# Rebasing float64 weights to float32: a parametric ReLU on ScalarE and two VectorE steps in place of three or four

## The chip, the cores and the metric

The kernel runs on one core of a Trainium2 chip. The core has five engines that run side by side, each through its own instructions in a fixed order: TensorE (PE in the profile) for matrix products, VectorE (DVE), ScalarE (ACT) and GpSimd (POOL) for elementwise work, and SyncE (SP), whose queue issues the transfers between the chip's main memory and the on-chip memory. The metric is the device time of one execution in microseconds (us); lower is better.

## The reference

Eight batches of eight heads of attention with a local window and 32 global positions, and then a gated feed-forward network over the 4608 rows that come out:

```python
# attention, per batch and head: D = 64, Sl = 512 local and Sg = 32 global positions
k_all, v_all = concat(k_g, k_l), concat(v_g, v_l)
out_g = softmax(q_g @ k_all.T / 8) @ v_all
mask = abs(pos[:, None] - pos[None, :]) <= 32
s_l = concat(q_l @ k_g.T / 8, where(mask, q_l @ k_l.T / 8, -1e9))
out_l = softmax(s_l) @ v_all
x = concat(out_g, out_l)                      # as (4608, 512)
# feed-forward: d_model = 512, d_ff = 1536
gate = 1.0 / (1.0 + np.exp(-(x @ w_gate)))
val = x @ w_val
return (gate * val @ w_out).astype(np.float32)
```

The three weight matrices are drawn as float32 and then multiplied by a float64 scalar, so they arrive as float64.

## The kernel before

**Weights.** A float64 weight reaches the kernel as two 32-bit words: `high` (sign, 11 bits of exponent, upper 20 bits of mantissa) and `low` (the rest). The kernel makes a float32 of the two, and splits that into a rounded part `hi` and a remainder `lo`, which TensorE multiplies in its faster float32 format in three passes (hi·hi, lo·hi, hi·lo).

There are 36 pieces to convert, 12 blocks f of each of w_gate, w_val and w_out, in the order gate, val, out for f = 0, 1, ... A piece is a tile of 128 x 1024 words, and its words become 128 x 512 float32. The sources are loaded by SyncE into three buffers in turn (`stage`, line 126; `in_w_gate_dram`, `in_w_val_dram` and `in_w_out_dram` in the profile); the load for piece i + 3 is issued after piece i has been read. The results `v` have two buffers in turn. All five buffers are parts of one tile, called `xt` in the profile, as the tiles are that hold the input of the feed-forward.

`convert(i, hi, lo)` does these steps, all on `high` and `low` with a stride of two words:

1. L137, VectorE: `v = high & 0x80000000`, the sign.
2. L141 on ScalarE for odd i, or L143 on VectorE for even i: `high`, read as a float32, is multiplied in place by 2^-112. Read so, the upper 8 of the 11 exponent bits are a float32's exponent, and the multiplication takes 112 from them, which takes 896 = 1023 - 127 from the float64's exponent.
3. L144, VectorE: `v = (low >> 29) | v`, the lowest three bits of the mantissa.
4. L145, VectorE: `v = (high << 3) | v`. The shift drops the sign and the two exponent bits that are zero by now.
5. L146, ScalarE: `hi = round(v)`; L147, GpSimd: `lo = v - hi`. For gate and val these go to the resident tiles `wg` and `wv`; for out they go to two temporary tiles and from there by SyncE to main memory (`wo_dram`, L158 and L159), from which every block is loaded again (L433) when it is used.

**Work around it.** The rows are taken in chunks: 256 rows, 256 rows, then seven chunks of 512, and the 256 global rows last. Attention for a chunk runs ahead of the feed-forward of that chunk, mixed into the feed-forward of earlier chunks. One unit of local attention is: scores on TensorE (`bank_x`, L239), mask and maximum on VectorE (L253), exponential on ScalarE (L256, also its sum), reciprocal on VectorE (L259, L260), normalisation into `p_buf` (L223 on VectorE or L221 on ScalarE), transposes on TensorE (`bank_y`, L275), a copy of them on ScalarE (`pt_nat`, L283, in the first chunks), the product with the values on TensorE (L298, L299), and a copy of the result on ScalarE (L302). Global positions have the like (L323 to L361). The feed-forward of one block f is 12 matmuls for the gate (`bank_g`, L405), 12 for the value (`bank_v`, L405), tanh, exponential and absolute value on ScalarE (L413 to L420), two VectorE steps (L425, L426), the split into `hh` (L428 ScalarE, L429 VectorE), and the product with w_out (`bank_o`, L442). While the first chunk's attention runs alone, `fill` (L110) issues matmuls of no use that keep TensorE going.

**Order.** The kernel keeps a queue of events by due time, counted in units of four 512-column matmuls, and emits those that are due between the feed-forward's groups of matmuls. Conversions of block 0 come during the first chunk's attention, the others at four units a block:

```python
CONVERT = (-2, 4, 1, 3)
CONVERT_EARLY = (-985, -980, -977)
```

From what is emitted, the framework's planner, which has costs of its own for every instruction, fixes the order on each engine and sets the waits. `tc.issue_after(x)` tells it to put the instructions inside the block behind x on x's engine; for the first three pieces, `convert` does so with `anchor[0]`, the last masked score (L253) emitted, which is on VectorE.

Of the kernel before, what the change touches and what calls it, by code (L numbers as in the profile page):

```python
# [11 lines left out]
AF = mybir.ActivationFunctionType  # L12
ALU = mybir.AluOpType
# [38 lines left out]
REBASE = "vs"  # L52
# [7 lines left out]
def kernel(ctx, tc, qk, v, w_gate, w_val, w_out, out_l, out_g):  # L60
    nc = tc.nc
# [60 lines left out]
    def stage(i):  # L122
        if i < len(w_src):
            src = w_src[i]
            st = conv_bufs[0][i % len(conv_bufs[0])].rearrange("p (t n) -> p t n", t=src.shape[1])
            nc.sync.dma_start(st, src)

    def convert(i, hi, lo):

        src = w_src[i]  # L130
        t, n = src.shape[1], src.shape[2] // 2
        st, v = (o[i % len(o)].rearrange("p (t n) -> p t n", t=t) for o in conv_bufs)
        words = st.rearrange("p t (n two) -> p t n two", two=2)
        low, high = words[:, :, :, 0], words[:, :, :, 1]
        vf, hf = v.bitcast(F32), high.bitcast(F32)
        with tc.issue_after(anchor[0].ins) if i < 3 else nullcontext():
            nc.vector.tensor_scalar(v, high, 0x80000000, None, op0=ALU.bitwise_and)  # L137


            if REBASE[i % len(REBASE)] == "s":  # L140
                nc.scalar.mul(hf, hf, 2.0 ** -112)  # L141
            else:
                nc.vector.tensor_scalar(hf, hf, 2.0 ** -112, None, op0=ALU.mult)  # L143
            nc.vector.scalar_tensor_tensor(v, low, 29, v, op0=ALU.logical_shift_right, op1=ALU.bitwise_or)  # L144
            nc.vector.scalar_tensor_tensor(v, high, 3, v, op0=ALU.logical_shift_left, op1=ALU.bitwise_or)  # L145
        nc.scalar.copy(hi, vf)  # L146
        nc.gpsimd.tensor_tensor(lo, vf, hi.bitcast(F32), op=ALU.subtract)  # L147
        stage(i + len(conv_bufs[0]))

    def convert_w(f, i):  # L150
        fs = slice(f * P, (f + 1) * P)
        w = (wg, wv)[i]
        convert(3 * f + i, w[0][:, :, fs], w[1][:, :, fs])

    def convert_wo(f):
        hi, lo = (spl.tile([P, 1, DM], F32R, name=nm, tag="kl") for nm in ("wo_hi", "wo_lo"))
        convert(3 * f + 2, hi, lo)
        nc.sync.dma_start(wo_dram[f][:, 0], hi[:, 0].bitcast(F32))  # L158
        nc.sync.dma_start(wo_dram[f][:, 1], lo[:, 0].bitcast(F32))  # L159
# [463 lines left out]
```

## Time and profile before

| | |
|---|---|
| runs: median (lowest to highest of 3) | 1196.94 us (1195.49 to 1201.54) |
| the profiled execution | 1196.95 us, with a span of 1195.2 us from its first to its last instruction |
| TensorE busy | 1154.4 us, 97% of the span |
| weight loads of TensorE (PEld) | 967.4 us, 81% |
| VectorE busy | 808.8 us, 68% |
| ScalarE busy | 746.6 us, 62% |
| GpSimd busy | 416.6 us, 35% |
| mean granted clock of TensorE | 0.992 of full |
| moved by DMA | 151.81 MB, 127 GB/s in the mean |

The profile's lines name the source line (L144), the engine, the operation, the tile written and, behind the arrow, those read. A group's line ends with its busy time, the mean of one in ns, and the idle time of the engine just before, with what ended it. "A <- B" in a list of waits says that A waited and B let it go. The queue of an engine carries a q (SPq is SyncE's). The granted clock is the share of its full clock that TensorE was given.

### The profile page before, as it was taken

The page shows a single profiled execution, that of the slowest core. Times are in us where ns is not written, and L with a number is a line of the kernel's source. Part 1 is how long each engine was busy: PE and PEld are TensorE (multiplying, and loading weights), DVE is VectorE, ACT ScalarE, POOL GpSimd, SP SyncE. Part 2 cuts the span into 40 slices and gives each one's busy share as a digit, 9 for nine tenths or more (in the row PEclk, how much of TensorE's full clock was granted, in tenths as well). Part 3 has the DMA queues.
Part 4 walks back from the last instruction along what each step waited for, and adds up shares of the span by engine and source line. Part 5 has one row for each costly group of instructions (what it writes and reads, how often), then busy time and mean ns, then how long its engine had stood idle before and what let it go on. Part 6 is the DMA issues. An engine that isn't in the chain of part 4 may idle for free.

```text
span 1195.2 us, 19155 instructions
## 1 busy us (share of the span) xinstructions
PE 1154.4 (97%) x6596; PEld 967.4 (81%) x6596; DVE 808.8 (68%) x2186; ACT 746.6 (62%) x1719; POOL 416.6 (35%) x408
## 2 busy tenths in 40 slices
PE   8889999999999999999999999999999999999998
PEld 6667778888888888888888888888888888888897
DVE  6989966766776776766776776667676677633343
ACT  4776777756765676766676666666665666532333
POOL 1335344524442444424443444434443443100000
PEclk9899999999999999999999999999999999999999
DMA  8787854333433443434333433443343342132143
GB/s 289 240 258 230 261 173 136 114 101 98 123 95 119 126 111 88 123 119 114 99 111 115 123 98 108 114 128 96 114 114 102 114 114 67 53 106 64 61 145 120
DMA packets 59489, 151.81 MB, mean 127 GB/s; under 512 B 6144, under 2 KB 19456, under 8 KB 59392
## 3 DMA queue, kind: packets, MB, share of 16 engines
q1 hardware_dynamic: 59392, 150.59, 41.8%
q8 instruction: 52, 0.85, 0.3%
q14 instruction: 45, 0.37, 0.1%
HBM read 135.36 MB, written 15.20 MB: 126 GB/s over the span
## 4 chain that ended last, share of the span: by engine, by line
PE 76%; DVE 13%; ACT 6%; issue 3%; DMA 1%; POOL 0%; ACTq 0%; SPq 0%; DVEq 0%; POOLq 0%
PE bank_v L405 20%; PE bank_g L405 20%; PE bank_o L442 19%; PE bank_x L239 4%; DVE p_buf L223 4%; PE bank_y L275 4%; ACT s_sb L256 2%; PE bank_x L323 2%; PE bank_x L306 2%; PE bank_x L307 2%; PE bank_x L366 1%; DVE bank_v L425 1%; DVE bank_v L426 1%; DVE mn L418 1%; DVE t L310 1%
## 5 line engine op out<-in xcount | busy, mean ns | idle before, releaser
L405 PE MATMUL bank_v<-xt,wv 128*128 128x512 f32 (+1 forms) x1440 | 329.9, 366 | 14.1 <-DVE pt L287 14.1
L405 PE MATMUL bank_g<-xt,wg 128*128 128x512 f32 (+1 forms) x1440 | 332.3, 366 | 0.6 <-ACT pg_buf L327 0.6
L442 PE MATMUL bank_o<-wo,hh 128*128 128x512 f32 x1224 | 328.9, 400 | 0.9 <-ACT hh L428 0.5
L405 PEld LDWEIGHTS bank_v<-xt,wv 128*128 128x128 f32 x1440 | 238.9, 191 | 51.3 <-issue 16.2
L405 PEld LDWEIGHTS bank_g<-xt,wg 128*128 128x128 f32 x1440 | 238.4, 190 | 38.1 <-issue 3.1
L442 PEld LDWEIGHTS bank_o<-wo,hh 128*128 128x128 f32 x1224 | 217.1, 189 | 40.7 <-ACT hh L428 1.4
L256 ACT ACTIVATE s_sb<-s_sb,nm 128x192 f32<-128x192 f32 (+1 forms) x240 | 110.4, 461 | 100.5 <-DVE nm L253 99.6
L223 DVE TENSOR_SCALAR p_buf<-s_sb,r 128x128 f32<-128x128 f32 (+2 forms) x443 | 154.8, 386 | 6.1 <-PE bank_y L275 1.7
L311 POOL TENSOR_TENSOR x<-t 64x256 f32<-64x256 f32 x104 | 76.4, 735 | 172.4 <-DVE t L310 148.4
L216 POOL TENSOR_TENSOR vhl<-v_raw,vhl 128x512 fp32r<-128x512 f32 x52 | 67.2, 1293 | 187.8 <-ACT vhl L215 88.1
L203 POOL TENSOR_TENSOR kl<-qk_raw,qk_hi 128x704 fp32r<-128x704 f32 x52 | 88.6, 1705 | 108.2 <-ACT qk_hi L202 107.7
L428 ACT CAST hh<-bank_v 128x512 fp32r<-128x512 f32 (+1 forms) x120 | 62.7, 523 | 95.4 <-DVE bank_v L426 94.6
L413 ACT ACTIVATE th<-bank_g 128x512 f32<-128x512 f32 (+1 forms) x120 | 63.9, 532 | 88.0 <-PE bank_g L405 87.5
L418 DVE TENSOR_SCALAR mn<-bank_g 128x512 f32<-128x512 f32 (+1 forms) x108 | 67.5, 625 | 72.3 <-ACT th L413 72.3
L310 DVE TENSOR_TENSOR t<-bank_x,t 64x512 f32<-64x512 f32 x104 | 70.7, 680 | 62.1 <-ACT t L309 61.1
L425 DVE TENSOR_TENSOR bank_v<-bank_v,mn 128x512 f32<-128x512 f32 (+1 forms) x120 | 73.6, 614 | 51.5 <-PE bank_v L405 48.2
L253 DVE CUSTOM_DVE_ANT_0 s_sb<-bank_x,masks 128x192 f32<-128x192 f32 (+1 forms) x240 | 80.0, 370 | 38.1 <-PE bank_x L239 35.1
L429 DVE TENSOR_TENSOR hh<-bank_v,hh 128x512 fp32r<-128x512 f32 (+1 forms) x120 | 73.0, 608 | 34.8 <-ACT hh L428 32.7
L205 POOL TENSOR_TENSOR qk_hi<-qk_raw,qk_hi 64x256 fp32r<-64x256 f32 x104 | 80.2, 792 | 4.1
L275 PE MATMUL bank_y<-ident,p_buf 128*128 128x128 f32 x440 | 70.7, 276 | 6.5 <-DVE p_buf L223 5.6
L426 DVE SCALAR_TENSOR_TENSOR bank_v<-th,bank_v 128x512 f32<-128x512 f32 (+1 forms) x120 | 73.2, 610 | 1.6
L275 PEld LDWEIGHTS bank_y<-ident,p_buf 128*128 128x128 f32 x440 | 54.8, 141 | 22.6 <-DVE p_buf L223 5.7
(110 smaller groups left out, 1694.6 us busy)
## 6 DMA issues: line engine op xcount, KB each, us to landing
wo<-wo_dram SPq DMA_DIRECT2D x116, 512.0 KB, 3.4
qk_raw<-in_qk_dram SPq DMA_DIRECT2D x104, 312.0 KB, 4.5
v_raw<-in_v_dram SPq DMA_DIRECT2D x52, 256.0 KB, 2.6
out_dram<-ob SPq DMA_DIRECT2D x34, 256.0 KB, 3.0
xt<-in_w_gate_dram SPq DMA_DIRECT2D x12, 512.0 KB, 4.8
xt<-in_w_val_dram SPq DMA_DIRECT2D x12, 512.0 KB, 4.6
xt<-in_w_out_dram SPq DMA_DIRECT2D x12, 512.0 KB, 4.7
v_nat<-in_v_dram SPq DMA_DIRECT2D x8, 512.0 KB, 6.2
```

Source lines behind the costliest of these rows:

```text
L203: nc.gpsimd.tensor_tensor(kl, t[:, K0:Q1], hi[:, K0:Q1].bitcast(F32), op=ALU.subtract)
L205: nc.gpsimd.tensor_tensor(hi[64:128, r], t[64:128, r], hi[64:128, r].bitcast(F32), op=ALU.subtract)
L223: nc.vector.tensor_scalar(out, in_, by, None, op0=ALU.mult)
L253: anchor[0] = nc.vector.tensor_tensor_reduce(out=s_sb[:, i, w], in0=s_ps[:, i, w], in1=mid[:, w], scale=-0.125, scalar=3.0e38, op0=ALU.add ...
L256: exp_at[0] = nc.scalar.activation(s_sb[:, i, w], s_sb[:, i, w], AF.Exp, bias=nm[:, i:i + 1], scale=-1.0, accum_out=sm[:, i:i + 1])
L275: nc.tensor.transpose(pt_ps[:, t], flat[:, t * P:(t + 1) * P], ident)
L310: nc.vector.tensor_tensor(t0, o_ps[0:64], t0, op=ALU.add)
L405: nc.tensor.matmul(acc, w[a][:, t, fs], xt[:, c, t, x0:x0 + ntok], start=n == 0, stop=n == 11)
L418: nc.vector.tensor_scalar(mn, acc, 0.0, None, op0=ALU.min)
L425: nc.vector.tensor_tensor(acc, acc, mn, op=ALU.mult)
L426: nc.vector.scalar_tensor_tensor(acc, th, 1.0, acc, op0=ALU.add, op1=ALU.mult)
L442: nc.tensor.matmul(o_ps[t], ph[:, a, t * P:(t + 1) * P], pwo[:, c], start=f2 == 0 and i == 0, stop=f2 == NF - 1 and i == 2)
```

## The change

Steps 1 and 3 above lose the sign, and step 2 runs on ScalarE for every piece. It is a parametric ReLU: it scales `high` by 2^-112 and, where the result is negative, multiplies by -2^32. That leaves a positive number whose 8 exponent bits are 32 higher than without the sign; 32 is bit 28 of the word, and the shift by 3 of step 4 lifts it to bit 31, the sign of a float32. So `v` starts as `low >> 29`, with no OR. The ReLU stands ahead of the `issue_after` block. What follows (L146, L147, the next load) is as it was; the number of transfers is too.

```diff
         vf, hf = v.bitcast(F32), high.bitcast(F32)
+        nc.scalar.activation(hf, hf, AF.Prelu, scale=2.0 ** -112, alpha=-2.0 ** 32)
         with tc.issue_after(anchor[0].ins) if i < 3 else nullcontext():
-            nc.vector.tensor_scalar(v, high, 0x80000000, None, op0=ALU.bitwise_and)
-
-
-            if REBASE[i % len(REBASE)] == "s":
-                nc.scalar.mul(hf, hf, 2.0 ** -112)
-            else:
-                nc.vector.tensor_scalar(hf, hf, 2.0 ** -112, None, op0=ALU.mult)
-            nc.vector.scalar_tensor_tensor(v, low, 29, v, op0=ALU.logical_shift_right, op1=ALU.bitwise_or)
+            nc.vector.tensor_scalar(v, low, 29, None, op0=ALU.logical_shift_right)
             nc.vector.scalar_tensor_tensor(v, high, 3, v, op0=ALU.logical_shift_left, op1=ALU.bitwise_or)
         nc.scalar.copy(hi, vf)
         nc.gpsimd.tensor_tensor(lo, vf, hi.bitcast(F32), op=ALU.subtract)
```

## The prediction

> **What bounds the kernel now.** I read the page first, then the stretches of the run, then TensorE's waits in the one stretch that the change touches, then the groups of VectorE and ScalarE there.
>
> ```profile
> span 1195.2 us, 19155 instructions
> ...
> PE   8889999999999999999999999999999999999998
> ...
> DVE  6989966766776776766776776667676677633343
> ```
>
> Each digit is a fortieth of the span, about 30 us. TensorE (PE) is at 9 nearly throughout: a TensorE-bound kernel. Only its first three digits are 8, and there VectorE (DVE) reads 9 8 9 9 behind its first 6, against 6 and 7 later. That is where the weights are converted. The next view gives stretches in us; its columns are TensorE, weight loads, VectorE, ScalarE and GpSimd busy time (instructions), then the granted clock, the DMA share and GB/s.
>
> ```profile
> 20.00:40.00 20.00, 16.47 (x97) 12.23 (x95) 19.35 (x57) 13.31 (x34) 7.15 (x7) 0.90 0.69 229
> 40.00:60.00 20.00, 19.76 (x107) 15.17 (x107) 17.32 (x45) 15.39 (x45) 7.81 (x7) 0.84 0.74 241
> ...
> 80.00:100.00 20.00, 18.23 (x97) 13.89 (x96) 15.42 (x38) 14.74 (x42) 7.16 (x6) 0.83 0.64 208
> ...
> 20.00:160.00 140.00, 125.81 (x786) 97.03 (x785) 127.28 (x317) 101.81 (x281) 56.03 (x43) 0.94 0.76 244
> ...
> 300.00:1000.00 700.00, 685.86 (x3787) 575.02 (x3787) 494.54 (x1371) 465.86 (x1023) 288.78 (x285) 1.00 0.39 111
> ```
>
> From 20 to 160 us TensorE stands idle for 140 - 125.81 = 14.2 us, while VectorE is busy for 127.28 of 140 (91%) and ScalarE for 101.81 (73%). In 300 to 1000 us, with VectorE at 71% (494.54 of 700) and ScalarE at 67%, TensorE idles 2%: nothing to win there by this change, which touches nothing there. There is a second loss in the early stretch, the clock: 0.10 of 16.47, 0.16 of 19.76 and 0.17 of 18.23 make 1.6 + 3.2 + 3.1 = 7.9 us that TensorE would not need at full clock. So the most that the stretch can give is 14.2 + 7.9 = 22.1 us, and the floor is about 1175 us. Who makes TensorE wait in 20 to 160 us (total us, times, longest):
>
> ```profile
> PE bank_y L275 <- DVE p_buf L223: 5.6, 5, 2.2
> PE bank_x L298 <- ACT pt_nat L283: 3.1, 4, 1.8
> PE bank_y L345 <- DVE r L259: 1.5, 1, 1.5
> PE bank_x L298 <- ACT pt_first L283: 0.7, 1, 0.7
> PE bank_g L405 <- ACT pg_buf L327: 0.6, 1, 0.6
> PE bank_y L275 <- ACT pg_buf L327: 0.6, 1, 0.6
> PE bank_y L275 <- DVE p_first L223: 0.5, 1, 0.5
> PE bank_x L360 <- ACT ptg_nat L349: 0.5, 1, 0.5
> PE bank_o L442 <- ACT hh L428: 0.5, 1, 0.5
> PE bank_o L442 <- DVE hh L429: 0.4, 1, 0.4
> PE bank_y L275 <- ACT p_buf L221: 0.2, 1, 0.2
> ```
>
> VectorE ends 5.6 + 1.5 + 0.5 + 0.4 = 8.0 us of them, ScalarE 6.2 us; together all of the 14.2. None names a converted weight (wg, wv): TensorE never waits for a conversion itself, but for softmax steps that stand behind conversion steps in VectorE's order.
>
> **The change part by part.** The groups of the conversion in 20 to 160 us (busy us, mean ns), VectorE's four and ScalarE's:
>
> ```profile
> L145 DVE SCALAR_TENSOR_TENSOR xt<-xt 128x512 uint32<-128x512 uint32 x36 | 30.9, 860 | 1.1 <-ACT xt L141 0.5
> L144 DVE SCALAR_TENSOR_TENSOR xt<-xt 128x512 uint32<-128x512 uint32 x35 | 30.2, 862 | 0.2
> L137 DVE TENSOR_SCALAR xt<-xt 128x512 uint32<-128x512 uint32 x35 | 19.5, 558 | 4.0 <-POOL wv L147 2.3 <-POOL wo_lo L147 1.2 <-DMA xt<-in_w_val_dram 0.4
> L143 DVE TENSOR_SCALAR xt<-xt 128x512 f32<-128x512 f32 x17 | 10.1, 595 | 0.1
> ...
> L141 ACT ACTIVATE xt<-xt 128x512 f32<-128x512 f32 x18 | 12.3, 681 | 2.7 <-DVE xt L137 2.6
> L146 ACT CAST wg<-xt 128x512 fp32r<-128x512 f32 x12 | 7.4, 619 | 3.6 <-DVE xt L145 3.2
> ```
>
> *VectorE.* The mask (L137) becomes a shift of the low words: one tensor-scalar, same tile, same stride, so I take 558 ns again, no gain. It still waits for GpSimd's subtraction two steps back, since v has two buffers: the 2.3 + 1.2 us of waits in its row stay. L144 goes (30.2 us) and L143 goes (10.1 us). VectorE drops by 40.3, from 127.3 to 87.0 us.
>
> *ScalarE.* Today it multiplies in 18 of the 36 conversions (12.3 us); afterwards it runs a parametric ReLU in all 36, on the same strided tile, in place. No such instruction is in the trace. Nearest is L141 itself, an ACTIVATE with a scale on the same tile: 681 ns, which I take. The casts of the same size (619) bound it below; above I take the widest ACTIVATE, 128x544 with a bias column, 750 ns. So 36 x 0.681 = 24.5 us, 12.2 more than now (10.0 to 14.7); ScalarE goes from 101.8 to 114.0 us, 81% of 140, or 88% if the stretch shrinks to 130.
>
> ```profile
> L337 ACT ACTIVATE pg_buf<-pg_buf,mg 128x544 f32<-128x544 f32 x16 | 12.0, 750 | 1.8 <-DVE mg L336 1.8
> ```
>
> The Trainium skill (ScalarE: Activation LUTs, "Rules for kernel authors") speaks against this part: multiplies and ReLUs belong on VectorE. The rows agree on the price, 595 ns there against 681 here; the 17 moved multiplies would cost 17 x 0.086 = 1.5 us more in engine time by that rule, and the sum would only turn if VectorE had the idle time, which here it has not.
>
> *Waits.* The multiply waited for VectorE's mask (2.6 us of ScalarE's idle time in L141's row); the ReLU does not. One case of it is in the order of time (start, duration; idle before):
>
> ```profile
> 79.23 1.49 DVE L137 TENSOR_SCALAR xt<-xt 128x512 uint32<-128x512 uint32 x1 [1.16 <-POOL wv L147]
> ...
> 80.75 0.71 ACT L141 ACTIVATE xt<-xt 128x512 f32<-128x512 f32 x1 [1.99 <-DVE xt L137]
> ...
> 82.20 0.43 PE L298 MATMUL bank_x<-pt_nat,v_nat 128*64 128x128 f32 x2 [1.77 <-ACT pt_nat L283]
> ```
>
> GpSimd holds the mask, the mask holds ScalarE's multiply, behind which stands the copy of transposed probabilities (L283), for which TensorE waits 1.8 us; the clock then falls (0.83 in 80 to 100). That chain is cut. In exchange the ReLU is now the first to wait for the weight load, on ScalarE, with exponentials (L256), copies (L283, L302), tanh (L413) and the cast behind it, and VectorE's last step behind these. Today the first step waits for a load once, 0.4 us in L137's row, here:
>
> ```profile
> 111.73 0.38 SPq L126 DMA_DIRECT2D xt<-in_w_val_dram  x1
> ...
> 117.98 0.43 DVE L137 TENSOR_SCALAR xt<-xt 128x512 uint32<-128x512 uint32 x1 [0.39 <-DMA xt<-in_w_val_dram]
> ```
>
> The load took about 6.2 us from issue, VectorE ran late behind it, and TensorE's longest wait for p_buf, 2.2 us, follows. That one I leave in. No DMA is added or removed; a load is released by the conversion's last step, which comes about one L144 (0.86 us) sooner, so SyncE's queue gains a little, nothing that TensorE waits for. The ReLU also stands outside the ordering block of the first three conversions, so ScalarE may take it earlier in the first chunk of attention; at worst it holds one exponential for its own 0.68 us, three times, 2.0 us in all, at best nothing; I take nothing, as these fill copies of L110 run on TensorE there.
>
> *The sum.* (1) VectorE's 8.0 us of waits: all but the 2.2 go, since 40.3 of 127.3 us leave its order: 5.8 (bounds 3 to 8.0). (2) ScalarE's 6.2: the 1.8 goes; the rest grows with 12.2 us more work in the same order. If a sixth of that lands in front of something that TensorE needs, it costs 2.0 (bounds 0 and about 6, half of it; I stay low because TensorE now waits only 6.2 us for an engine at 73%): net -0.2. (3) Clock: 3.1 us of 80 to 100 go with their cause; of the 4.8 us in 20 to 60, which follow the first chunk's gaps (3.5 us idle in 20 to 40), I take a quarter, 1.2: 4.3 (bounds 1 to 7.9). Together 9.9 us. The profiled execution took 1196.95 us, 1.75 over its span and equal to the median of the runs (1196.94), so 1187.0 us.
>
> The Trainium skill (TensorE: Matmul & The Clock Gate, "Part 1: The HAM clock gate") says that the clock halves after an idle window of about 3.4 us. No gap in the rows is that long (longest 2.2), and the clock fell all the same; by the rule there would be nothing to recover and the sum would be 5.6 us, 1191.3, which is counted with rival A. The rows decide.
>
> **The rivals.**
> (A) Latency, not load: TensorE's waits are turns of the softmax loop, and ScalarE takes VectorE's place as the full engine. For it: 6.2 of the 14.2 us are ScalarE's already, at 73%. Against it: TensorE idles 2% in 300 to 1000 us with the same kind of loop and both engines near 70%. Half of the 8.0 goes (4.0), ScalarE takes 2.0 back, the clock gives 1: 1194, within the 0.5% (6 us, 1191 to 1203) that a measurement of this kernel can tell from no change.
> (B) Slower: ScalarE is held by weight loads. 36 conversions in 140 us are one per 3.9 us; with three buffers a load has two periods, 7.8 us, less the conversion in front. Against the median load of 4.6 us below that leaves about 3 us, against the 6.2 above next to nothing. It decides where loads take over 7.8 us: if half of the 36 hold ScalarE for 2.0 us, as L137 held it at 80.75, 36 us come on top of 114.0 and ScalarE needs 150 us for a stretch of 140: 10 us longer, 1207.
>
> ```profile
> xt<-in_w_val_dram SPq DMA_DIRECT2D x12, 512.0 KB, 4.6
> ...
> L256 ACT ACT_TABLE_LOAD x1 | 1.3, 1283 | 0.7 <-PEq L610 0.7
> ```
>
> (C) The parametric ReLU may not be in the table set that the exponentials and tanh share, which the program loads once. Two loads round each conversion are 72 x 1.283 = 92 us on ScalarE: 206 us for a stretch of 140, 66 us longer, 1263. Relu, abs, exp and tanh here share one load, which speaks against it. The Trainium skill (ScalarE: Activation LUTs, "Table sets: the hidden batching unit") names relu and abs as fillers of every set and does not name this function, and gives a switch 2.66 us with its drain, by which it would be worse.
> (D) More: all of VectorE's 8.0, the 1.8 and the whole 7.9 of clock, 17.7 us: 1179.
>
> **How the numbers follow.** Forecast 0.48 (its own range 1181 to 1191), A 0.27, B 0.11, C 0.03, D 0.11 (1175 to 1181). Faster by over 0.5%: 0.48 + 0.11 = 0.59; within: 0.27; slower: 0.14. The range 1177 to 1203 leaves out B, C and the lower third of D, 0.18. The point is the forecast's, 1187.
>
> **What would show it.** Right: L144's and L143's work gone, VectorE near 87 us of the stretch, one ScalarE activation of about 0.68 us per conversion, one table load, TensorE's waits for p_buf under 3 us, the clock at 1.00 in 80 to 100, and the conversions over some 10 us sooner. Wrong: ScalarE waiting for in_w loads (B), waits for ScalarE's copies grown by what VectorE's lost (A), a slow clock after the first chunk as before with no gap removed, or a ReLU much over 0.75 us.

## The result, and the profile after

The changed kernel takes 1187.33 us (median of 6 runs, 1185.29 to 1191.53), the kernel before 1197.34 us on the same chip (6 runs, 1195.49 to 1201.54). The ratio is 0.9916, with a 95% interval of 0.9893 to 0.994: 0.84% faster, 10 us. The profiled execution of the changed kernel took 1188.97 us, with a span of 1187.1 us, 8.1 less than the span before.

Lines of the changed kernel are 6 less than those of the kernel before from L145 on (L145 is now L139, L223 is L217, L405 is L399), the parametric ReLU is L136 and the shift that takes the mask's place L138. The page's head, and its slices of about 30 us:

```profile
span 1187.1 us, 19115 instructions
...
DVE  5767756666776676667776677677676677633343
ACT  5897777666666666666666666576665675532333
```

VectorE's first digits are 5 7 6 7 7 5 where they were 6 9 8 9 9 6. ScalarE's third is 9 now. The stretches of the changed kernel (TensorE, weight loads, VectorE, ScalarE, GpSimd busy; clock; DMA):

```profile
20.00:40.00 20.00, 17.45 (x112) 13.35 (x110) 16.56 (x48) 14.41 (x39) 8.90 (x8) 1.00 0.83 269
40.00:60.00 20.00, 19.20 (x120) 14.78 (x120) 13.30 (x42) 18.01 (x52) 7.61 (x8) 1.00 0.83 270
...
80.00:100.00 20.00, 18.15 (x106) 12.84 (x107) 12.38 (x36) 18.68 (x50) 6.94 (x7) 1.00 0.80 259
100.00:120.00 20.00, 18.02 (x123) 13.78 (x121) 14.28 (x35) 12.58 (x36) 8.35 (x7) 0.86 0.73 239
...
20.00:160.00 140.00, 130.62 (x845) 100.87 (x844) 98.31 (x273) 114.09 (x313) 56.59 (x47) 0.98 0.79 256
...
300.00:1000.00 700.00, 686.37 (x3788) 575.47 (x3787) 494.69 (x1373) 463.41 (x1018) 290.81 (x290) 1.00 0.38 111
```

In 20 to 160 us TensorE idles for 9.4 us instead of 14.2, and gets 845 matmul records done instead of 786. The clock is full up to 100 us, where three of these stretches were slow before (0.90, 0.84 and 0.83); it falls once, later, in 100 to 120. In 300 to 1000 us nothing has changed. That nearly everything was won early shows in the stores of the result, of the kernel before and of the changed one (the last two numbers are the start of the first and the last store):

```profile
L387 SPq DMA_DIRECT2D out_dram<-ob x34: 332/342/426, 246.5 to 1192.1; - x34
```
```profile
L381 SPq DMA_DIRECT2D out_dram<-ob x34: 332/360/433, 238.7 to 1184.0; - x34
```

The first is 7.8 us sooner, the last 8.1. Who makes TensorE wait in 20 to 160 us of the changed kernel:

```profile
PE bank_y L269 <- DVE p_buf L217: 2.7, 3, 1.1
PE bank_x L292 <- ACT pt_nat L277: 1.1, 1, 1.1
PE bank_y L269 <- ACT mn L409: 1.0, 1, 1.0
PE bank_o L436 <- ACT hh L422: 0.9, 1, 0.9
PE bank_y L339 <- DVE r L253: 0.8, 1, 0.8
PE bank_g L399 <- DVE hh L423: 0.8, 1, 0.8
PE bank_x L292 <- ACT pt_first L277: 0.7, 1, 0.7
PE bank_y L269 <- ACT p_buf L215: 0.5, 1, 0.5
PE bank_y L269 <- DVE hh L423: 0.2, 1, 0.2
PE bank_y L339 <- DVE pg_buf L217: 0.2, 1, 0.2
```

VectorE ends 4.7 us of them (8.0 before), ScalarE 4.2 (6.2 before). The steps of the conversion in the changed kernel, first VectorE's in the whole run, then ScalarE's by the source line (min/median/max in ns, first and last start):

```profile
L139 DVE SCALAR_TENSOR_TENSOR xt<-xt 128x512 uint32<-128x512 uint32 x36 | 30.0, 837 | 7.4 <-ACT xt L136 7.0
```
```profile
L138 DVE TENSOR_SCALAR xt<-xt 128x512 uint32<-128x512 uint32 x36 | 21.3, 596 | 11.7 <-POOL wo_lo L141 4.9 <-POOL wg L141 3.0 <-DMA xt<-in_w_gate_dram 1.8
```
```profile
L136 ACT ACTIVATE xt<-xt x36: 647/676/694, 8.7 to 145.3; 128x512 f32<-128x512 f32 x36
L136 ACT ACT_TABLE_LOAD  x1: 1283/1283/1283, 0.7 to 0.7; - x1
```

The ReLU costs what the multiplication did (676 ns), and one table load serves the program. Something that the prediction had seen only in part is at the very start. ScalarE in the kernel before, and in the changed one:

```profile
6.15 0.46 ACT L256 ACTIVATE s_first<-s_first,nm 128x192 f32<-128x192 f32 x1 [4.13 <-DVE nm L253]
```
```profile
8.69 0.68 ACT L136 ACTIVATE xt<-xt 128x512 f32<-128x512 f32 x1 [6.67 <-DMA xt<-in_w_gate_dram]
9.27 0.44 ACT L250 ACTIVATE s_first<-s_first,nm 128x192 f32<-128x192 f32 x1
```

The planner puts the first ReLU ahead of the first exponential. ScalarE waits there 6.67 us for the weight load, and the first exponential starts 3.1 us later than before. TensorE hardly feels it: its dummy matmuls (L110) run meanwhile, and its first product with the values (L298 before, L292 now) starts at 13.79 us, where it started at 13.34.

### The profile page after: what moved, and what is told of

Read it like the earlier page. It is cut to its first block, busy times and chain, and to the rows that moved or that the text cites. A ratio compares the mean times of both kernels' runs of the same rounds, so it can differ in the third digit from the quotient of the medians.

```text
span 1187.1 us, 19115 instructions
## 1 busy us (share of the span) xinstructions
PE 1150.8 (97%) x6596; PEld 963.8 (81%) x6596; DVE 776.9 (65%) x2132; ACT 755.0 (64%) x1737; POOL 412.4 (35%) x408
## 4 chain that ended last, share of the span: by engine, by line
PE 70%; DVE 10%; ACT 5%; issue 2%; POOL 1%; DMA 0%; ACTq 0%; DVEq 0%; POOLq 0%
PE bank_v L399 19%; PE bank_g L399 19%; PE bank_o L436 19%; DVE p_buf L217 4%; PE bank_y L269 3%; PE bank_x L233 3%; ACT s_sb L250 3%; PE bank_x L300 2%; PE bank_x L301 2%; PE bank_x L317 1%; PE bank_x L360 1%; DVE t L304 1%; DVE mn L412 1%; DVE bank_v L419 1%; DVE bank_v L420 1%
## 5 line engine op out<-in xcount | busy, mean ns | idle before, releaser
L399 PE MATMUL bank_v<-xt,wv 128*128 128x512 f32 (+1 forms) x1440 | 327.8, 364 | 14.7 <-DVE pt L281 14.4
L399 PE MATMUL bank_g<-xt,wg 128*128 128x512 f32 (+1 forms) x1440 | 331.1, 365 | 1.1 <-DVE hh L423 0.8
L399 PEld LDWEIGHTS bank_v<-xt,wv 128*128 128x128 f32 x1440 | 237.0, 189 | 51.8 <-issue 16.4
L399 PEld LDWEIGHTS bank_g<-xt,wg 128*128 128x128 f32 x1440 | 237.3, 189 | 38.7 <-issue 2.7
L217 DVE TENSOR_SCALAR p_buf<-s_sb,r 128x128 f32<-128x128 f32 (+2 forms) x443 | 152.4, 381 | 6.3 <-PE bank_y L269 1.7
L413 ACT ACTIVATE mn<-mn 128x512 f32<-128x512 f32 (+1 forms) x108 | 62.9, 582 | 15.8 <-DVE mn L412 11.1
```

Of the source, the lines that this page charges most:

```text
L217: nc.vector.tensor_scalar(out, in_, by, None, op0=ALU.mult)
L399: nc.tensor.matmul(acc, w[a][:, t, fs], xt[:, c, t, x0:x0 + ntok], start=n == 0, stop=n == 11)
```

## The experiments

The theory is the prediction's: TensorE waits early on for softmax steps that stand behind conversion steps in VectorE's order, and the gain is VectorE's shorter order ("load"). The rivals: the gain is that ScalarE's step no longer waits for VectorE's mask ("chain"); it is the planner's new order ("order"); it is TensorE's clock ("clock"). Ratios are to the kernel before on the same chip; the mean clock is that of a kernel's runs. The kernel before had 0.992 in each of the three sets of runs.

| kernel | median us (runs) | ratio (95% interval) | mean clock |
|---|---|---|---|
| changed | 1187.33 (6) | 0.9916 (0.9893 to 0.994) | 0.998 |
| or_again | 1195.22 (12) | 0.9972 (0.9957 to 0.9987) | 0.995 |
| scalar_twice | 1199.87 (12) | 1.0003 (0.9986 to 1.002) | 0.992 |
| mul_all_scalar | 1197.03 (12) | 0.9993 (0.9978 to 1.0007) | 0.994 |
| mul_all_vector | 1201.50 (12) | 1.0024 (1.0011 to 1.0037) | 0.991 |
| more_fill_before | 1205.28 (6) | 1.0048 (1.003 to 1.0066) | 0.994 |
| prelu_odd | 1195.94 (12) | 0.9973 (0.9959 to 0.9988) | 0.994 |
| prelu_late | 1179.82 (4) | 0.9836 (0.9816 to 0.9857) | 0.999 |
| norm_vector | 1186.75 (5) | 0.9887 (0.9869 to 0.9905) | 0.999 |
| shifted_before | 1198.97 (12) | 1.0002 (0.9982 to 1.0023) | 0.992 |
| shifted_after | 1188.99 (6) | 0.9921 (0.9898 to 0.9944) | 0.997 |
| late_or_again | 1198.46 (12) | 0.9999 (0.998 to 1.0018) | 0.992 |
| norm_late | 1184.04 (6) | 0.9879 (0.9854 to 0.9904) | 0.998 |

### VectorE's step put back (or_again)

```diff
             nc.vector.tensor_scalar(v, low, 29, None, op0=ALU.logical_shift_right)
+            nc.vector.scalar_tensor_tensor(v, low, 29, v, op0=ALU.logical_shift_right, op1=ALU.bitwise_or)
```

> The changed kernel with VectorE's OR-shift of the low words put back behind the plain shift (it gives the same words again). ScalarE's parametric ReLU stays, so nothing on ScalarE waits for VectorE's mask. VectorE gets back 36 instructions of about 0.86 us, 30 of the 40 us that the change took off it. Load theory (the gain is VectorE's order made shorter): three quarters of the loss of TensorE waits comes back, 1193 to 1197 us, and TensorE's waits for VectorE in 20 to 160 us go back over 6 us. Chain theory (the gain is that ScalarE's multiply no longer waits for VectorE): stays within 2 us of the changed kernel, 1186 to 1190.

Measured: ratio 0.9972, so 0.56% of the 0.84% is gone: 0.0056 x 1197 = 6.7 us for 30 us of VectorE. Its stretch from 20 to 160 us:

```profile
20.00:160.00 140.00, 125.56 (x808) 97.28 (x807) 120.81 (x302) 110.36 (x299) 59.17 (x45) 0.96 0.79 252
```

VectorE is at 120.8 us, and TensorE's idle time is back to 14.4, of which VectorE ends 7.4. No mask stands ahead of ScalarE's step here, and yet most of the gain is lost: load, not chain. The step put back also makes each conversion longer by some 0.86 us, which this run doesn't separate from the load.

### The multiplications on one engine (mul_all_scalar, mul_all_vector)

```diff
-REBASE = "vs"
+REBASE = "s"     # mul_all_scalar; "v" in mul_all_vector
```

> The kernel before with all 36 multiplications on ScalarE, none on VectorE; mask and both OR-shifts stay on VectorE. VectorE loses 10 us, ScalarE gains 12.2, and all 36 ScalarE multiplications wait for VectorE's mask where 18 did. Load theory: a quarter of the VectorE term, 1 to 2 us faster, less 2 for ScalarE: 1195 to 1199. Chain theory: twice as many waits of ScalarE behind the mask, slower, 1199 to 1203.

> The kernel before with all 36 multiplications on VectorE: VectorE gains 10.5 us in the early stretch, ScalarE loses 12.3, and nothing on ScalarE waits for the mask any more. Load theory: VectorE is over 95% busy there, slower by 3 to 8 us, 1200 to 1205. Chain theory: faster, 1192 to 1196.

Measured: 0.9993, not to be told from the kernel before, and 1.0024, slower by 0.24% (2.9 us), at the lower end of what load expected. In the second nothing on ScalarE waits for the mask any more, and ScalarE has 12 us less to do; chain expected a gain. It is refuted as the main cause. No conversion has a step more there, so these 2.9 us speak for VectorE's load by itself. mul_all_scalar and or_again have the same work on both engines and differ in whether ScalarE's step waits for VectorE's: 0.9993 against 0.9972. The intervals overlap, so a share of the order of 0.2% for the chain is neither shown nor excluded; late_or_again below, which has the same work again and no mask ahead of ScalarE's step either, is at 0.9999 and shows no gain for it.

### Half of the change (prelu_odd)

```diff
+        if i % 2:
+            nc.scalar.activation(hf, hf, AF.Prelu, scale=2.0 ** -112, alpha=-2.0 ** 32)
+            ...
+        else:
             ...
```

> Half of the change: odd pieces use the parametric ReLU and two VectorE steps, even pieces the old four VectorE steps. ScalarE has the same 18 instructions as before, none of them waiting for the mask any more; VectorE loses 18 OR-shifts, 15 us. Load theory with the slope so far (30 us put back cost 6.7 us): 3 to 4 us faster than before, 1194 to 1196. Chain theory (what counts is that ScalarE's step doesn't wait for VectorE): nearly the whole gain, 1188 to 1191.

Measured: 0.9973. ScalarE's work is that of the kernel before, no step of it waits for a mask, and 15 of VectorE's 40 us are gone (38%): a third of the gain (0.27 of 0.84). That is load's number, and not chain's.

### ScalarE's price (scalar_twice)

```diff
         nc.scalar.activation(hf, hf, AF.Prelu, scale=2.0 ** -112, alpha=-2.0 ** 32)
+        nc.scalar.mul(hf, hf, 1.0)
```

> The changed kernel with one more ScalarE instruction a conversion, a multiplication of the rebased words by 1.0 in place: 36 x 0.68 = 24.5 us more on ScalarE, which then has about 138 us in a stretch of 130 to 140. This measures what ScalarE's added time costs, which the prediction put at a sixth (2.0 us for 12.2). By the prediction's sixth: 4 us over the changed kernel, 1191. By the rival that ScalarE takes VectorE's place as the full engine: 8 us or more over it, 1195 to 1203.

Measured: 1.0003. The whole gain is gone: 0.0087 x 1197 = 10.4 us for 24.5 us more on ScalarE, 0.43 us for each, where the prediction had a sixth. That is the time which the rival of ScalarE as the full engine forecast. Its stretch, of an execution that was the slowest of the 12 (1203.28 us):

```profile
20.00:160.00 140.00, 125.13 (x779) 98.59 (x777) 85.64 (x249) 119.51 (x313) 48.53 (x41) 0.93 0.76 244
```

VectorE is at 85.6 us, less than anywhere else, and TensorE idles 14.9 us. By the list of its waits VectorE ends 7.2 of them, ScalarE 4.7 and loads of `wo` 2.0. VectorE isn't short of time here; its last conversion step waits 13.0 us for ScalarE's, 7.0 in the changed kernel. So ScalarE's added step costs the 10 us, but that ScalarE is full isn't shown: prelu_late below has it busier in this stretch (122.18 us), and TensorE idles 4.8 us there. The added step also makes each conversion longer by 0.68 us, which this run doesn't separate from the load.

### Another order of the same work (shifted_before, shifted_after)

```diff
-CONVERT = (-2, 4, 1, 3)
+CONVERT = (-1.5, 4, 1, 3)
```

> The kernel before with the conversions of blocks 1 to 11 due half a unit (about 0.8 us) later; same instructions, another order from the planner. It measures how much a new order alone moves the time. Load theory: within 2 us of the kernel before, since no engine's work changes. Order rival (the 10 us are the luck of a new order): 4 us or more in either direction.

> The same half unit later in the changed kernel. Load theory: 7 to 12 us below the kernel before with the same shift, as the change is without it. Order rival: the gain over the shifted kernel before shrinks under 4 us or vanishes.

Measured: 1.0002 and 0.9921. The change is worth the same 10 us (1198.97 to 1188.99) when the conversions fall due elsewhere. As far as this one shift goes, the gain isn't the luck of an order; prelu_late below is an order that moves the time a good deal more.

### The clock (more_fill_before)

```diff
-FILL = (8, 1)
+FILL = (8, 3)
```

> The kernel before with three dummy matmuls instead of one at each of the places in the first chunk's attention where TensorE has nothing to do (the second number of FILL). Nothing of the conversion is touched. Over the runs so far, time and granted clock move together: the kernel before has 0.988 to 0.994 in the mean of its runs, the changed one 0.995 to 1.000. Clock theory (most of the gain is that shorter gaps no longer bring the clock down): the two slow stretches in 20 to 60 us go, mean clock to 0.995 or 0.996, 3 to 5 us faster, 1194 to 1196. Idle theory (the gain is TensorE's waits, and the clock is a symptom that costs nothing by itself, since work at a slow clock only fills waits): the clock may rise, the time stays within 1.5 us or grows by the dummies, 1197 to 1201.

Measured: slower, 1.0048. The dummies do hold the clock at full in 20 to 60 us (0.90 and 0.84 before), but they fill TensorE to the last (20.00 of 20.00 in 20 to 40) and the real work is later (the last exponential of the first chunk starts at 37.9 us, 31.8 before):

```profile
20.00:40.00 20.00, 20.00 (x148) 17.24 (x147) 15.90 (x51) 11.79 (x33) 8.00 (x7) 1.00 0.58 189
40.00:60.00 20.00, 15.13 (x102) 12.06 (x101) 17.52 (x43) 12.37 (x33) 8.00 (x7) 1.00 0.73 239
```

So the run doesn't price the clock. The runs of single kernels don't settle it either. A line through the 12 runs of scalar_twice, mul_all_scalar or mul_all_vector falls by 0.77 to 0.82 us for each 0.001 of mean clock, but the same line falls by 0.28 for or_again, by 1.4 for shifted_before and, in the three sets of the kernel before, by 0.86 to 1.9. The mean clock of the kernel before is 0.992, that of the changed one 0.998: by these lines 2 to all of the 10 us go with the 6 thousandths. Whether the clock makes that time or shorter gaps make both stays open.

### The first three ReLUs behind the exponentials (prelu_late)

```diff
-        nc.scalar.activation(hf, hf, AF.Prelu, scale=2.0 ** -112, alpha=-2.0 ** 32)
+        with tc.issue_after(exp_at[0].ins) if i < 3 else nullcontext():
+            nc.scalar.activation(hf, hf, AF.Prelu, scale=2.0 ** -112, alpha=-2.0 ** 32)
```

> The changed kernel with the ReLUs of the first three pieces put behind the last exponential emitted (an ordering edge on ScalarE, as the two VectorE steps have it on theirs). In the profile of the changed kernel the first ReLU makes ScalarE wait 6.7 us for its weight load, with the first four exponentials behind it, which start at 9.3 us where they started at 6.2. If that matters, 0.5 to 2 us faster than the changed kernel, 1185 to 1187; if the dummy matmuls cover it, no difference.

Measured: 1179.82 us, ratio 0.9836, far more than expected: 0.0080 x 1197 = 9.6 us below the changed kernel (by the two ratios), as much again as the change itself. The first exponential is back at 6.07 us. But the gain doesn't stand there. Two products with the values and the first matmul of the feed-forward, in the changed kernel and in this one:

```profile
29.99 0.43 PE L292 MATMUL bank_x<-pt_first,v_nat 128*64 128x128 f32 x2
...
35.12 0.43 PE L292 MATMUL bank_x<-pt_nat,v_nat 128*64 128x128 f32 x2 [1.10 <-ACT pt_nat L277]
...
38.49 0.62 PE L399 MATMUL bank_g<-xt,wg 128*128 128x256 f32 x3
```
```profile
29.93 0.43 PE L293 MATMUL bank_x<-pt_first,v_nat 128*64 128x128 f32 x2
...
32.62 0.43 PE L293 MATMUL bank_x<-pt_nat,v_nat 128*64 128x128 f32 x2 [1.03 <-ACT pt_nat L278]
...
35.99 0.62 PE L400 MATMUL bank_g<-xt,wg 128*128 128x256 f32 x3
```

Up to 30 us the two run level, so ScalarE's wait for the first load costs TensorE next to nothing. Then this kernel gets 2.5 us ahead: in the changed one VectorE takes 2.91 us from 29.84 us on for four normalisations, and TensorE waits 0.78 us for them and 1.10 for the copy behind; here VectorE takes 1.51 us for the four. The rest is won after that. The stretch:

```profile
20.00:160.00 140.00, 135.18 (x905) 106.08 (x904) 99.66 (x291) 122.18 (x336) 61.67 (x50) 1.00 0.83 264
```

TensorE idles 4.8 us, at full clock throughout, with 905 matmul records. Both engines have the changed kernel's instructions. So this is the same work in another order, and this order is worth as much as the change. The edge moves three ReLUs and, through the planner, what follows them; where the 9.6 us come from wasn't separated, and the same edge is worth nothing clear of noise in the next two kernels that have it.

### The same step put back there (late_or_again)

The edits of prelu_late and or_again together.

> The changed kernel with the first three ReLUs put behind the last exponential emitted (1179.8 us) and VectorE's OR-shift of the low words put back, 30 us of VectorE. Load theory: slower than without the OR-shift by about the 7 us that the same step cost in the changed kernel, 1185 to 1189. If it was the order of the first pieces that VectorE's load had spoilt there: under 3 us, 1180 to 1183.

Measured: 0.9999, the time of the kernel before. The same 30 us of VectorE that cost 0.56% in the changed kernel cost 1.63% here, 19.5 us, nearly three times what was expected, and neither range was hit:

```profile
20.00:160.00 140.00, 123.56 (x763) 96.23 (x763) 118.48 (x293) 107.63 (x291) 51.76 (x42) 0.92 0.74 241
```
```profile
PE bank_y L271 <- DVE p_buf L219: 5.3, 4, 2.0
```

With VectorE at 118.5 us, TensorE waits for p_buf again, idles 16.4 us, and the clock is at 0.92. Beside or_again, which differs by the edge alone, nothing is gained: 0.9999 with it, 0.9972 without (the intervals overlap), though the first exponential starts at 6.1 us here and at 8.9 there. So what the edge gained in prelu_late isn't the price of the wait at the start, and it hangs on the short VectorE order. In direction it is load's result; why the price of the step triples stays open.

### Normalisations moved to VectorE (norm_vector, norm_late)

```diff
-NORM = {0: "v", 1: "v", 2: "ssv", 3: "sv"}
+NORM = {0: "v", 1: "v", 2: "v", 3: "v"}
```

> The changed kernel with the normalisations of the second chunk and of the first heads of the third all on VectorE (they are two thirds and one half on ScalarE). It moves about 11 us of the early stretch from ScalarE (114 us there) to VectorE (98). If ScalarE is now the engine that TensorE waits for: 2 to 4 us faster than the changed kernel, 1183 to 1186. If VectorE's order is still what counts: slower, 1188 to 1192.

> Both small edits together in the changed kernel: the first three ReLUs behind the last exponential emitted, and the normalisations of the second chunk and of the first heads of the third all on VectorE. If both act by themselves (8 and 3 us): 1176 to 1178. If they work on the same waits: 1179 to 1181. If VectorE's added 11 us count more with TensorE better fed: over 1182.

Measured: 0.9887 on the changed kernel, 3.5 us faster by the two ratios, but the intervals overlap (0.9869 to 0.9905 and 0.9893 to 0.994), so a gain isn't settled. What load expected here, 1188 to 1192 us, is missed: VectorE is at 113.65 us in 20 to 160 (98.31 in the changed kernel), and the kernel isn't slower. On prelu_late it is slower by the middle values, 0.9879 against 0.9836 (the intervals just overlap), as was expected if VectorE's added work counts more there; beside norm_vector the edge gains 0.0008, within the noise. The traces suggest why norm_late is slower than prelu_late: TensorE waits for VectorE's normalisations again, 6.4 us of p_buf against 0.3. They show more than the middle values do, since norm_late's execution was the slowest of its six (1188.01 us) and prelu_late's the fastest of its four (1178.23).

```profile
PE bank_y L270 <- DVE p_buf L218: 6.4, 7, 1.9
```
```profile
PE bank_y L270 <- DVE p_buf L218: 0.3, 1, 0.3
```

The fastest kernel of the study is prelu_late, 1179.82 us: below both.

## Why the prediction was right, and where its terms were off

The place, the sign and the size came out: 1187.0 forecast, 1187.33 measured, nearly all of it before the first store. Step by step:

- *VectorE's work.* 40.3 us were to go in 20 to 160 us. By durations of the whole run L144 (30.8) and L143 (10.5) are gone, L138 is 1.4 more than L137 was, and L145's successor 0.9 less: 40.8. Right. Busy time fell less, from 808.8 to 776.9 us, because records of instructions back to back overlap. The forecast of 87 us in the stretch didn't hold (98.3): the stretch holds more of the other work now.
- *Why it pays.* Waits behind VectorE's order: TensorE waits 2.7 us for p_buf where it waited 5.6, and or_again, prelu_odd and mul_all_vector go the way that load forecast, with the rival chain refuted as the main cause. How the shorter order pays is in part argued. or_again and prelu_odd change the length of a conversion together with VectorE's load, norm_vector gave VectorE other work and wasn't slower, and prelu_late shows an order of the same work that is worth as much as the change, where the one shift tested moved nothing. Term 1 was put at 5.8 us; VectorE's part of TensorE's waits fell by 3.3 in the profiled execution. Too large there.
- *ScalarE's ReLU.* 681 ns taken, 676 measured; one table load, so rival C is out. The Trainium skill's rule (ScalarE: Activation LUTs, "Rules for kernel authors") to keep such steps on VectorE was no guide here: mul_all_vector, which follows it for the multiplications, is the slower one (1.0024 against 0.9993).
- *ScalarE's price.* Term 2 was a loss of 0.2 us: 1.8 gained, 2.0 lost as a sixth of the added work. In the profiled execution ScalarE's part of TensorE's waits fell by 2.0 instead, though ScalarE came to the 114 us forecast. The sixth isn't confirmed by that: scalar_twice measured 0.43 for work added on top, by which the change's own 12.2 us would cost 5.2. What they cost stays open.
- *The first three ReLUs.* "I take nothing" came out near enough, and for the reason given, but the 2.0 us called the worst were not: they counted the ReLU's own duration and forgot that the ReLU waits for its load in ScalarE's order. Rival B named that wait, and looked for it in the steady part, where it hardly occurs (1.4 us of ScalarE's idle time in 20 to 160). It stands at the start, 6.67 us. The dummies that the prediction counted on covered it: TensorE's first product with the values is 0.45 us later than before and 0.06 us later than in prelu_late.
- *Clock.* 4.3 us taken. In the profiled pair the loss fell from 7.9 us to 0.14 x 18.02 = 2.5 in 100 to 120 us and some 0.6 in the 20 us behind, so by 4.8. What the clock is worth by itself stays open. It didn't go only where it was forecast: 20 to 60 us is at full clock too, and a new slow stretch came at 115 us.

So the sum was right in part by luck, since its errors stood against each other. TensorE's idle time in 20 to 160 us fell by 4.8 us where 5.6 were forecast, with VectorE's part 2.5 too high and ScalarE's 2.2 too low, and the clock gave 4.8 for 4.3. That the middle value lies 0.3 us from the forecast says little either: the runs of the changed kernel spread over 6 us.

## What to carry to other kernels

When a step moves to another engine, look at what its first instances wait for and what stands behind them there, and then whether the engine that bounds the kernel feels it: here ScalarE waited 6.67 us for a load, and TensorE's dummies covered it. Two engines that alternate in one loop have a price each, and it is no constant: the same 30 us of VectorE cost 6.7 us in one kernel and 19.5 in another. Measure it by putting an idempotent step in, which leaves the result as it is, and remember that such a step lengthens each pass through the loop as well as the load. An ordering edge on three instructions moved as much time as the change itself, so try more than one order before a gain is put down to the work taken away. A TensorE that waited in many short gaps lost clock as well here, so count both before saying what the most is that a stretch can give.

## What the runs showed of the hardware

The clock fell without a long gap. In the changed kernel (start, duration; idle before):

```profile
110.14 1.57 POOL L141 TENSOR_TENSOR wg<-xt,wg 128x512 fp32r<-128x512 f32 x1 [2.73 <-ACT wg L140]
...
110.84 2.19 DVE L217 TENSOR_SCALAR p_buf<-s_sb,r 128x128 f32<-128x128 f32 x2
...
111.68 1.26 POOL L141 TENSOR_TENSOR wv<-xt,wv 128x512 fp32r<-128x512 f32 x1
...
113.08 0.33 PE L269 MATMUL bank_y<-ident,p_buf 128*128 128x128 f32 x1 [0.79 <-DVE p_buf L217]
```
```profile
115.00:120.00 5.00, 5.00 (x17) 3.25 (x15) 2.60 (x9) 2.53 (x9) 1.27 (x1) 0.50 0.14 23
```

TensorE waited 1.1 and 0.79 us for p_buf, and from 115 to 120 us it had half its clock. Two such normalisations took 0.48 us at 115.56 us, with GpSimd idle, and 2.19 us here, beside two of GpSimd's subtractions; four of them, at 29.84 us, took 2.91 us beside two subtractions in the changed kernel, and 1.51 us beside one in prelu_late. L138's 36 run from 412 to 1512 ns around a median of 420. That VectorE's one-source steps are slowed while GpSimd works is what these rows suggest; no run here tested it.
